# Attention with a gated layer behind it: remainder blocks as 64x64 tiles, the layer's products in scaled float16 halves, the row sums folded into the probabilities, and a new order

## The chip, the cores and the metric

The kernel runs on one core of one Trainium2 chip. The metric is device microseconds (us) of one execution, as the median of several runs. The engines are named as the profile names them: PE multiplies matrices and PEld loads its stationary operand, DVE, ACT and POOL work on elements, and SP issues the DMAs. Each engine runs its own list of instructions in the order in which it stands, and waits on semaphores where it needs another engine's result.

## What is computed

Eight batches, eight heads, 576 positions, head size 64, all float32:

```python
scores = scale * np.matmul(q, k.transpose(0, 1, 3, 2))
psi_rel = np.log1p(np.abs(pos[:, None] - pos[None, :]))
psi_i = np.log1p(np.maximum(pos[:, None], 1.0))
bias = np.maximum((psi_rel / psi_i)[..., None] @ w1 + b1, 0.0) @ w2   # one per head, the same in every batch
attn = softmax(scores + bias)            # rows minus their maximum; 1e-9 is added to each row sum
x = concat over heads of attn @ v        # (8, 576, 512)
gate = sigmoid(causal convolution of x over 5 positions, a weight for each channel)
out = (gate * (x @ w_val)) @ w_out
```

## The kernel before

The work is cut into 32 *pairs*: two heads of one batch. One pair has 1152 rows of scores, in four blocks of 128 positions by two heads, and a *remainder* block for the last 64 positions of both heads.

**A block.** `qkm` (L623) makes the scores on PE with four float32 products that use 64 rows of the array each, two beside each other. `logits` (L665) adds the bias on DVE and takes the row's extreme. `expo` (L677) takes the exponential on ACT and sums the rows. From there a pair goes one of two ways, set by a string of T and D, `TRANS`:

- T: DVE turns the sums into reciprocals (`eps` L701, `recip` L704), `norm` (L722) multiplies the probabilities with them on POOL or DVE, PE transposes them in float32 (`tp`, L762), ACT or DVE copies them out of PSUM, and float32 products with v follow (`piece`, L832).
- D: `top` (L245 on ACT, L249 on POOL) rounds the probabilities to float16, `rest` (L252) subtracts that to get the low half, a transposing DMA (L796) turns both round, and float16 products with v follow (also L832, three for one). The reciprocals come in afterwards: `rb` (L881; L914 for the remainder) spreads them over PSUM with a product, and `mu` (L891, L925) multiplies the result with them on DVE.

12 of the 32 pairs are T, 20 are D. `LDWEIGHTS` rows are PE's loads of the stationary operand.

**The remainder.** `qkr` (L635) multiplies a stationary operand that is block diagonal for the two heads (zeros are loaded with q and k) with 640 columns of k, so that half of the products are with zeros. Its bias tile has -1e30 in the places that are not wanted. DVE, ACT and POOL then work on 640 columns, 576 of which matter.

**The bias** is computed once in the first 65 us, in 36 strips of 16 rows (`relu` L346 on DVE and L344 on ACT, `bias_mm` L365 on PE, `bias_fin` L384/L386), written to DRAM, and loaded again as skewed tiles. Only the tiles of four heads lie in SBUF at a time. So the pairs run as: heads 0-3 of batches 0-3; heads 4-7 of all batches in the order 0, 4, 1, 5, ...; heads 0-3 of batches 4-7. The bias is loaded three times, and the half of a batch's x that is made long before the other goes to DRAM (`xs`, L928) and back (L955).

**The gated layer** of a batch runs when both its halves are there: the convolution (L1009, L1018; for the last batch L968 to L983), the sigmoid (L1030), then in two parts of 256 and 320 positions `split_hi`/`split_lo` of x into a float32r high and low half, `val` (L1075, three products for one), `gf` (L1085: times the gate), `ghi`/`glo`, `outp` (L1132, three products for one), `ote` (copy out of PSUM) and the store. The weights are read as float64 bits and rebuilt on DVE (L454 to L484) after the bias stage.

**What sets the order.** Every step is a task with a list of engines that could do it, a cost for each, and a priority: the pair's place times `PER`, plus an offset from a table (`PAIR_AT`, `MLP_AT`, `OFFS` by the step's name). A planner takes the tasks by these numbers, its own costs and the number of buffers (`BUFS`), and writes one fixed list for each engine.

```python
t3 = add([("A", 0.77)], expo, [t2], h + 1)
t4 = tp_ = add([("A", 0.58), ("V", 0.38), ("G", 0.66)], top, [t3, tp_ if a else None], h + 1.2, ...)
t5 = add([("G", 1.25), ("V", 0.68)], rest, [t4], h + 2, (), [eb])
```

Here A, V and G are ACT, DVE and POOL, the figures are the planner's costs, and the list after the function holds what the task waits for.

Of the kernel before, what the change touches and what calls it, by code (L numbers as in the profile page):

```python
# [39 lines left out]
RUNS = ((0, (0, 1, 2, 3)), (1, (0, 4, 1, 5, 2, 6, 3, 7)), (0, (4, 5, 6, 7)))  # L40
MLP_STEPS = 33
MLP_AT = (27, 17, 14, 9, 8, 19, 12, 70)
PAIR_AT = (1, 3, -1, 0, -0.5, -1, 2.5, -2.5, -4.5, -5, -0.5, -0.5, -0.5, 0.5, 2.5, -1.5, -2, -2.5, -2, 1.5, 1.5, 1, -2.5, -0.5, -1.5, -5, -5.5, -7, 0, 3, 0.5, 0.5)
TRANS = tuple(x == "T" for x in "TTTDTTTTDTTDDTDDDDDTDDTDDDDDDDDD")
BUFS = dict(w=13, d=5, pt=2, sp=2, ps=4, qk=2, rel=4, be=6, xp=2, xh=1, gh=1, gx=1)
RING = dict(er="w", hlr="w", raw="w", e="d", hl="d", xo="w", vt="w", ptr="w", gate="w", gf="w", ot="w", tt="ps", po="ps", pm="ps", cv="ps")
LOOK = dict(w=14.02, ps=60.04, d=6.72, be=3.8, gh=227.3, pt=9.76, xh=21.35, sp=1.22, xp=0.44)
# [13 lines left out]
PARTS = ((0, 256), (256, 320))  # L61
LEAST = float(np.array([0x38000000], np.uint32).view(np.float32)[0])
# [16 lines left out]
class Plan:  # L79
# [6 lines left out]
    def __init__(self, bufs):  # L86
        self.tasks, self.bufs = [], bufs

    def add(self, engines, fn, deps=(), pri=0.0, takes=(), uses=(), hold=0.5):
        pri += OFFS.get(getattr(fn, "func", fn).__name__, 0.0)  # L90
# [3 lines left out]
        name = getattr(fn, "func", fn).__name__  # L94
# [110 lines left out]
def attention_gated_mlp(  # L205
# [23 lines left out]
    for k in set(BUFS) & {"sp", "ps", "w", "d", "pt", "qk"}:  # L229
# [20 lines left out]

    def sub(e, out, in0, in1):
# [176 lines left out]
    users_of_bias = {}  # L428

    def load_bias(run, hg, l, c, pri):  # L430
# [3 lines left out]
        def bias_ld(e):  # L434
            if c < NM:
                SP.dma_start(biasm[l][c], bias_rows_of(c, 2 * p, 2))
            else:
                SP.dma_start(biasr[l][0:REM, 0:S], bias_rows_of(c, 2 * p, 1))
                SP.dma_start(biasr[l][REM:P, REM:RW], bias_rows_of(c, 2 * p + 1, 1))

        deps = stored[c] + users_of_bias.get((run - 1, l, c), [])
        return add([("S", 1.65 if c < NM else 0.9)], bias_ld, deps, pri)


    def double(b, raw, n):
        mp = pools["mp"]
# [787 lines left out]
```

## Time and profile before

| | |
|---|---|
| median of 3 runs | 747.57 us (747.43 to 747.65) |
| the profiled execution, span | 748.5 us |
| PE busy | 704.3 us, 94% |
| DVE busy | 583.9 us, 78% |
| ACT busy | 575.0 us, 77% |
| POOL busy | 481.9 us, 64% |
| SP's DMA queue | 83.6% of 16 DMA engines' span |
| granted TensorE clock, mean | 0.990 |

A row of the groups reads: line, engine, operation, what is written and read, shapes, how many | busy us of the group, mean ns of one | idle time of the engine just before them, and what ended most of it. A float32 product is two records for one instruction. Busy time of an engine is a union: instructions that overlap count once.

### The profile page before, as it was taken

How to read it: one execution, taken by the hardware profiler on the slowest of the kernel's cores; microseconds unless marked ns; L12 is line 12 of the kernel's file. 1: busy time of each engine (PE TensorE's matmuls, PEld its weight loads, DVE VectorE, ACT ScalarE, POOL GpSimd, SP SyncE). 2: the span in 40 equal slices, each digit the busy share in tenths (PEclk: the TensorE clock that was granted, in tenths of full speed). 3: DMA queues.
4: the chain of work that ended last, by engine and by line, in shares of the span. 5: the costliest groups of instructions: out<-in, count | busy, mean ns of one | idle time of the engine just before them, and what ended most of it. 6: DMA issues, size and time to landing. Idle time of an engine off the chain costs nothing.

```text
span 748.5 us, 17263 instructions
## 1 busy us (share of the span) xinstructions
PE 704.3 (94%) x6122; PEld 498.4 (67%) x6122; DVE 583.9 (78%) x1590; ACT 575.0 (77%) x1277; POOL 481.9 (64%) x553
## 2 busy tenths in 40 slices
PE   5768999999989999999999999999999899999997
PEld 2214666666566666687687677767777678688886
DVE  6996698988879979988588768977579889897431
ACT  6988577777778997898677976797767988985632
POOL 1003369556767866699874695668787787876842
PEclk9989999999999999999999999999999999999999
DMA  8888248569893897899999689899999999996211
GB/s 274 280 267 270 80 151 190 146 193 281 170 228 104 145 201 185 177 199 211 224 212 212 140 184 231 259 247 194 235 221 194 226 247 208 198 170 133 71 48 51
DMA packets 273221, 143.23 MB, mean 191 GB/s; under 512 B 243312, under 2 KB 243568, under 8 KB 273136
## 3 DMA queue, kind: packets, MB, share of 16 engines
q1 hardware_dynamic: 272992, 141.84, 83.6%
q8 instruction: 48, 0.79, 0.4%
q10 hardware_dynamic: 144, 0.29, 0.2%
q14 instruction: 37, 0.30, 0.1%
HBM read 56.77 MB, written 25.05 MB: 109 GB/s over the span
## 4 chain that ended last, share of the span: by engine, by line
PE 57%; DMA 12%; DVE 12%; ACT 10%; issue 4%; POOL 3%; SPq 0%; POOLq 0%; ACTq 0%; DVEq 0%
PE t_sp L623 13%; PE t_ps L832 11%; PE t_ps L1132 11%; PE t_ps L1075 9%; DMA t_pt<-t_d 6%; PE t_ps L762 4%; PE t_sp L635 4%; DVE t_d L665 3%; DMA bias_d<-t_be 3%; DVE t_ps L1018 3%; ACT t_d L677 2%; PE t_ps L904 2%; DMA t_w<-vd 1%; PE t_ps L881 1%; DVE rel L346 1%
## 5 line engine op out<-in xcount | busy, mean ns | idle before, releaser
L677 ACT ACTIVATE t_d<-t_d,nm 128x576 f32<-128x576 f32 x256 | 197.8, 774 | 56.9 <-DVE nm L665 54.9
L252 POOL TENSOR_TENSOR t_d<-t_d 128x576 f16<-128x576 f32 x160 | 209.8, 1324 | 45.7 <-ACT t_d L245 37.6
L665 DVE CUSTOM_DVE_ANT_0 t_d<-t_sp,bias 128x576 f32<-128x576 f32 x256 | 188.2, 750 | 22.1 <-PE t_sp L623 10.4
L623 PE MATMUL t_sp<-t_qk 64*128 64x288 f32 x1024 | 174.7, 431 | 6.1 <-DVE nm L665 5.5
L832 PE MATMUL t_ps<-t_pt,t_w 128*64 128x256 f16 (+1 forms) x1680 | 141.7, 309 | 5.0 <-DMA t_pt<-t_d 3.7
L722 POOL TENSOR_SCALAR t_d<-t_d,rinv 128x576 f32<-128x576 f32 x96 | 72.8, 769 | 106.5 <-DVE rinv L704 58.6
L623 PEld LDWEIGHTS t_sp<-t_qk 64*128 64x128 f32 x1024 | 99.0, 186 | 55.1 <-issue 17.4
L1018 DVE SCALAR_TENSOR_TENSOR t_ps<-t_xp,convw,t_ps 128x288 f32<-128x288 f32 x168 | 86.9, 518 | 3.4 <-ACT t_ps L1009 0.8
L1075 PE MATMUL t_ps<-xh,wv 128*128 128x320 f32 (+1 forms) x512 | 83.4, 300 | 0.2 <-ACT t_pt L245 0.2
L245 ACT CAST t_d<-t_d 128x576 f16<-128x576 f32 x113 | 75.1, 669 | 6.6 <-POOL t_d L252 3.0
L832 PEld LDWEIGHTS <-t_w 128*64 128x64 f16 x1200 | 61.1, 109 | 25.0 <-issue 22.2
L1075 PEld LDWEIGHTS t_ps<-xh,wv 128*128 128x128 f32 x512 | 71.6, 188 | 8.5 <-issue 4.7
L1132 PE MATMUL t_ps<-wo,gh 128*128 128x512 f32 x256 | 71.0, 409 | 1.0 <-ACT gh L245 1.0
L762 PE MATMUL t_ps<-ident,t_d 128*128 128x128 f32 x432 | 62.7, 280 | 2.5 <-POOL t_d L722 0.9
L762 PEld LDWEIGHTS t_ps<-ident,t_d 128*128 128x128 f32 x432 | 47.0, 140 | 23.5 <-issue 8.3
L245 ACT COPY t_pt<-t_ps 128x512 f32<-128x512 f32 (+1 forms) x98 | 48.6, 516 | 11.4 <-PE t_ps L762 11.2
L1132 PEld LDWEIGHTS t_ps<-wo,gh 128*128 128x128 f32 x256 | 45.3, 188 | 16.2 <-issue 4.3
L365 PE MATMUL t_ps<-rel,w 128*32 128x288 f32 (+17 forms) x352 | 40.4, 525 | 14.6 <-ACT t_be L384 11.6
L1085 DVE TENSOR_TENSOR t_w<-t_ps,t_w 128x256 f32<-128x256 f32 (+1 forms) x64 | 28.5, 452 | 30.7 <-PE t_ps L1075 28.2
L252 POOL TENSOR_TENSOR gl<-t_w,gh 128x256 fp32r<-128x256 f32 x52 | 39.6, 762 | 19.4 <-ACT gh L245 15.8
L245 ACT COPY t_w<-t_ps 128x512 f32<-128x512 f32 (+2 forms) x64 | 31.8, 503 | 22.0 <-PE t_ps L1132 20.7
L677 ACT ACTIVATION_READ_ACCUMULATOR t_d<-t_d,nm 128x1 f32 x256 | 48.6, 190 | 0.0
(115 smaller groups left out, 1167.5 us busy)
## 6 DMA issues: line engine op xcount, KB each, us to landing
t_qk<-qkd SPq DMA_DIRECT2D x32, 640.0 KB, 4.7
bias<-bias_d SPq DMA_DIRECT2D x24, 576.0 KB, 4.8
bias_d<-t_be SPq DMA_DIRECT2D x36, 295.5 KB, 4.6
out<-t_w SPq DMA_DIRECT2D x32, 256.0 KB, 2.6
t_w<-vd SPq DMA_DIRECT2D x20, 320.0 KB, 3.9
xs<-t_w SPq DMA_DIRECT2D x16, 288.0 KB, 3.4
t_xp<-xs SPq DMA_DIRECT2D x8, 576.0 KB, 4.6
t_w<-vn SPq DMA_DIRECT2D x12, 320.0 KB, 5.2
```

The lines of the kernel that those rows point to most:

```text
L245: A.copy(out=out, in_=in_)
L252: (V if e == "V" else G).tensor_tensor(out=out, in0=in0, in1=in1, op=ALU.subtract)
L365: T.matmul(pb[32 * g : 32 * g + 32, 0 : y - x], lhsT=w28, rhs=rel[g].t[:, x:y], start=True, stop=True, tile_position=(0, 32 * g),)
L623: T.matmul(ts[a][:, j, 0:hw], lhsT=qk.t[r, c * P : (c + 1) * P], rhs=qk.t[r, x : x + hw], start=True, stop=True,)
L665: V.tensor_tensor_reduce(out=part().rearrange("p (j f) -> p j f", j=2), in0=sp.t[:, :, 0 : w // 2], in1=bias.rearrange("p (j f) -> p j f", ...
L677: A.activation(out=part(), in_=part(), func=AF.Exp, bias=nms[c][:, a : a + 1], scale=-1.0, accum_out=sums[c][:, a, 0:1],)
L722: (G if e == "G" else V).tensor_scalar(out=t, in0=t, scalar1=rinvs[c][:, a : a + 1], scalar2=1.0, op0=ALU.mult, op1=ALU.mult,)
L762: T.transpose(t[:, k * P : (k + 1) * P], es[c].t[:, (k0 + k) * P : (k0 + k + 1) * P], ident)
L832: T.matmul(po.t[r, 0:256], lhsT=vt.t[:, v0 + t, r], rhs=pt[:, w, :, :] if tr else pt[:, :, w, :], start=(k == 0), stop=(k == 5 * len(prods ...
L1018: V.scalar_tensor_tensor(out=o, in0=x, scalar=cw, in1=t, op0=ALU.mult, op1=ALU.add)
L1075: T.matmul(pm.t[:, 0:w], lhsT=pools["wv"][wi][:, k, d * P : (d + 1) * P], rhs=xb.t[xi][:, k, 0:w], start=(q == 0 and k == 0), stop=(q == 2 ...
L1132: T.matmul(pm.t, lhsT=gb.t[gi][:, k, o : o + P] if o < 256 else gx.t[gi][:, k, :], rhs=pools["wo"][wi][:, k, :], start=(q == 0 and k == 0) ...
```

## The change

Five things change together.

1. **Remainders.** The remainders of the two pairs that are neighbours (same batch, four heads) form one block of 128 rows: rows 0-63 for the first pair, 64-127 for the second. `qkr` makes it with eight 64x64 products, four for each half of the columns, each with its own place in the array. From then on it is a block of 576 columns like the others; the block-diagonal zeros, the -1e30 and all 640-column steps of the scores go.
2. **Reciprocal inside the split.** In a D pair `eps` and `recip` now come straight after the exponentials, `top` multiplies with the reciprocal as it rounds, and `rest` multiplies and subtracts: one instruction on DVE, two on POOL (L262, L263), and only POOL is listed. `rb` and `mu` go. `eps` may run on POOL (L771).
3. **The gated layer in float16.** Both operands are scaled with powers and maxima so that two float16 halves hold them. New: a maximum over every v tile (L620, L634), a trip of one value per partition through DRAM for each batch (L1010, L1014), one for the weights (L568, L572), scales in `split_hi` (ACT with a scale, L1132), `split_lo` (now DVE only, L1137), `gf` (L1177) and `ote` (L1241), and a row maximum with scales on the rebuilt weights (L532 to L541). float16 products need their own LDWEIGHTS in the list.
4. **Bias resident, batches in turn.** The bias tiles of all eight heads stay in SBUF. After batches 0 and 1 (interleaved) every batch is done with all heads before the next. `xs` and the reloads go; the gated layer of batch 0 can start after pair 5.
5. **Order.** All planner numbers are new. `TRANS` has one letter for two pairs, 18 pairs are now T and 14 D; the weights are rebuilt during and right after the bias stage; `BUFS` changes (w 13 to 12, d 5 to 6, qk 2 to 3).

```diff
-RUNS = ((0, (0, 1, 2, 3)), (1, (0, 4, 1, 5, 2, 6, 3, 7)), (0, (4, 5, 6, 7)))
+RUNS = ((0, (0, 1)), (1, (0, 1))) + tuple((hg, (b,)) for b in range(2, 8) for hg in range(2))
-TRANS = tuple(x == "T" for x in "TTTDTTTTDTTDDTDDDDDTDDTDDDDDDDDD")
+TRANS = tuple(x == "T" for x in "TTTTDTDDTDTDTDTD")
-BUFS = dict(w=13, d=5, pt=2, sp=2, ps=4, qk=2, rel=4, be=6, xp=2, xh=1, gh=1, gx=1)
+BUFS = dict(w=12, d=6, pt=2, sp=2, ps=4, qk=3, rel=3, be=8, xp=2, xh=1, gh=1, gx=1)
...
-                t, hw = new(sps[0], [P, 2, 512], F32), RW // 2
+                ts, hw = [new(sp, [P, 2, 512], F32) for sp in sps], S // 2
                 for j in range(2):
-                    T.matmul(t[:, j, 0:hw], lhsT=qk.t[:, NM * P : QW], rhs=qk.t[:, QW + j * hw : QW + (j + 1) * hw], ...)
+                    for a, r in enumerate(halfs):
+                        for m, o in zip(both, halfs):
+                            q = m["qk"].t
+                            x = S + j * hw
+                            T.matmul(ts[a][o, j, 0:hw], lhsT=q[r, NM * P : S], rhs=q[r, x : x + hw], ...)
...
-                        copy(e, hl.t[:, 0, :] if c == NM else hl.t[:, 0, a, :], part())
+                        o, i, x = hl.t[:, 0, a, :], part(c, a), rinvs[c][:, a : a + 1]
+                        if e == "A":
+                            A.activation(out=o, in_=i, func=AF.Copy, scale=x)
...
-                        sub(e, f(1), part(), f(0))
+                        scaled(e, hl.t[:, 1, a, :], part(c, a), rinvs[c][:, a : a + 1], hl.t[:, 0, a, :], ALU.subtract)
...
-                    t5 = add([("G", 1.25), ("V", 0.68)], rest, [t4], h + 2, (), [eb])
+                        moved[c, x] = add([("G", 2.0)], partial(rest, a=x), [tp_], h + 1 + x, (), [eb])
...
+    def scaled(e, out, in0, s, in1, op):
+        if e == "V":
+            V.scalar_tensor_tensor(out=out, in0=in0, scalar=s, in1=in1, op0=ALU.mult, op1=op)
+        else:
+            G.tensor_scalar(out=in0, in0=in0, scalar1=s, scalar2=1.0, op0=ALU.mult, op1=ALU.mult)
+            G.tensor_tensor(out=out, in0=in0, in1=in1, op=op)
...
-            x = add([("P", 0.44)], rb, [last, rsum[g]], d + 1.2, (), [po])
-            x1 = add([("V", 0.34)], mu, [x0, x], d + 2, (), [po])
+            x1 = x0
...
-                        xb.t = [pools["mp"].tile([P, NK, 320], F32R, name=x, tag=x) for x in ("xh", "xl")]
+                        xb.t = [pools["mp"].tile([P, NK, 320], F16, name=x, tag=x) for x in ("xh", "xl")]
...
-                u = add([("V", 0.38), ("G", 0.75)], split_lo, [h], base + 0.3 * k + 0.2, (), [xp])
+                u = add([("V", 0.38)], split_lo, [h], base + 0.3 * k + 0.2, (), [xp])
...
-                    copy(e, ot.t, pm.t)
+                    x = bsc[:, b, 0:1] if o < 256 else oscx[:, b_pair : b_pair + 1]
+                    if e == "A":
+                        A.activation(out=ot.t, in_=pm.t, func=AF.Copy, scale=x)
```

Three places show what this does to the lists.

DVE in the first half of the bias stage, before (`rel` is `relu`, `t_be` is `bias_fin`):

```order
L346 TENSOR_SCALAR rel<-gt,sct,nb_129 128x464 x3
L346 TENSOR_SCALAR rel<-gt,sct,nb_129 128x448 x3
L346 TENSOR_SCALAR rel<-gt,sct,nb_129 128x432 x3
L346 TENSOR_SCALAR rel<-gt,sct,nb_129 128x416 x3
L386 TENSOR_SCALAR t_be<-t_ps,cadd 128x464
L346 TENSOR_SCALAR rel<-gt,sct,nb_129 128x400 x3
L346 TENSOR_SCALAR rel<-gt,sct,nb_129 128x384 x3
```

The same place after the change (L522 ends the rebuilding of the convolution's weights, L620 is the maximum over a v tile):

```order
L620 TENSOR_REDUCE vcol<-t_w 128x1
L369 TENSOR_SCALAR rel<-gt,sct,nb_142 128x464 x3
L369 TENSOR_SCALAR rel<-gt,sct,nb_142 128x448 x3
L369 TENSOR_SCALAR rel<-gt,sct,nb_142 128x432 x3
L522 TENSOR_TENSOR convw<-t_w 128x20
L620 TENSOR_REDUCE vcol<-t_w 128x1
L369 TENSOR_SCALAR rel<-gt,sct,nb_142 128x416 x3
L369 TENSOR_SCALAR rel<-gt,sct,nb_142 128x400 x3
L369 TENSOR_SCALAR rel<-gt,sct,nb_142 128x384 x3
L620 TENSOR_REDUCE vcol<-t_w 128x1
```

Maxima over v and steps of the weights' rebuilding (eight of 512 columns follow before the last strip) have moved in between the strips.

POOL in a D pair between two T pairs, before (`t_d` 128x576 on L252 is `rest`, on L722 `norm`):

```order
L252 TENSOR_TENSOR t_d<-t_d 128x576 x2
L252 TENSOR_TENSOR xl<-t_xp,xh 128x320 x2
L252 TENSOR_TENSOR t_d<-t_d 128x576 x2
L722 TENSOR_SCALAR t_d<-t_d,rinv 128x576 x2
L252 TENSOR_TENSOR t_w<-t_w 128x640
```

POOL at such a place after the change (L771 is `eps`, L820 `top`, L262 and L263 the two steps of `rest`, L799 `norm`):

```order
L771 TENSOR_SCALAR rinv<-sm_162 128x2
L262 TENSOR_SCALAR t_d<-t_d,rinv 128x576
L263 TENSOR_TENSOR t_d<-t_d 128x576
L262 TENSOR_SCALAR t_d<-t_d,rinv 128x576
L263 TENSOR_TENSOR t_d<-t_d 128x576
L820 TENSOR_SCALAR t_d<-t_d,rinv 128x576
L262 TENSOR_SCALAR t_d<-t_d,rinv 128x576
L263 TENSOR_TENSOR t_d<-t_d 128x576
L799 TENSOR_SCALAR t_d<-t_d,rinv 128x576 x2
```

Each low half is now two instructions on POOL; the low halves of x (`xl`) have left POOL.

ACT after the last remainder's copy (L922) at the end of the program, before:

```order
L922 ACTIVATE t_xp<-t_ps,vsc 128x64
L972 ACTIVATE t_w<-t_xp,convw 128x576
L245 CAST xh<-t_xp 128x320 x3
L245 COPY t_w<-t_ps 128x512
L245 CAST gh<-t_w 128x256
L245 COPY t_w<-t_ps 128x512
L245 CAST gh<-t_w 128x256 x2
L972 ACTIVATE t_w<-t_xp,convw 128x576
L978 ACTIVATE t_w<-t_xp,convw 128x576
L245 COPY t_w<-t_ps 128x512
```

The same place after the change (L975 is that copy, L1053 and L1059 the convolution, L1241 `ote`, L1111 the sigmoid):

```order
L975 ACTIVATE t_xp<-t_ps,vsc 128x64
L1053 ACTIVATE t_w<-t_xp,convw 128x576
L1241 ACTIVATE t_w<-t_ps,bsc 128x512
L1111 ACTIVATE t_w<-t_w 128x576
L1059 ACTIVATE t_w<-t_xp,convw 128x576
L1241 ACTIVATE t_w<-t_ps,bsc 128x512
L1059 ACTIVATE t_w<-t_xp,convw 128x576 x2
L249 CAST gh<-t_w 128x256
```

Less of the batch before the last is left to stand beside the last convolution: two output copies, where before a whole part of it and five copies followed.

More of the change, by code (lines that the diff above doesn't have):

```diff
@@ L506, in cw, with w_max, w_scale, w_inv @@
                 )
-            return add([("V", 0.1)], cw, [t], pri)
+            return add([("V", 0.1)], cw, [t], pri, (), tmp)
+        m = ("wv", "wo").index(hi_lo)
+        wm, wt, wi = (x[:, m, k : k + 1] for x in wrow)
+        def w_max(e):
+            V.tensor_reduce(out=wm, in_=b["a"].bitcast(F32), op=ALU.max, axis=AX.X, apply_absolute_value=True)
+        def w_scale(e):
+            scalars(e, wt, wm, 1e-30, 2.0**-12, ALU.max)
+        def w_inv(e):
+            V.reciprocal(out=wi, in_=wt)
@@ new lines, in attention_gated_mlp, with wg_store, wg_load, wg_max @@
+    last = WEIGHTS[0] + 9 * WEIGHTS[1]
+    wall, wallb = {}, Buf("wall")
+    def wg_store(e):
+        SP.dma_start(wbd, wrow[1].rearrange("p m k -> p (m k)"))
+    def wg_load(e):
+        wall["t"] = new(wallb, [P, P * 2 * NK], F32)
+        SP.dma_start(wall["t"], wbd.rearrange("p c -> (p c)").partition_broadcast(P))
+    def wg_max(e):
+        t = wall["t"].rearrange("q (p m k) -> q m p k", m=2, k=NK)
+        V.tensor_reduce(out=wsc[:, 0:2], in_=t, op=ALU.max, axis=AX.XY)
+    def wg_inv(e):
+        V.reciprocal(out=wsc[:, 2:4], in_=wsc[:, 0:2])
@@ L530, in attention_gated_mlp @@
     spilled, arrived, taker = {}, {}, {}
+    maxima = {}
+    mates = {}
     def pair(n):
@@ L611, in pair, with part, block @@
         hls = {}
-        for c in range(NM + 1):
-            w = S if c < NM else RW
-            sps = [Buf("sp") for _ in range(2 if c < NM else 1)]
+        mine = mates[n] = dict(qk=qk, loaded=loaded, vt=vt, tv=tv)
+        both = [mates[n - 1], mine] if l else None
+        ptr = Buf("ptr")
+        def part(c, a):
+            return es[c].t[:, a * S : (a + 1) * S]
+        def block(c):
+            exps = {}
+            sps = [Buf("sp") for _ in range(2)]
             def qkm(e, c=c, sps=sps):
@@ L703, in recip @@
+                    o = rinvs[c] if tr else sums[c][:, 1, :, 0]
+                    V.tensor_reduce(out=o, in_=sums[c][:, 0], op=ALU.add, axis=AX.X)
+                    if not tr:
+                        V.tensor_reduce(out=rinvs[c], in_=sums[c][:, 1], op=ALU.mult, axis=AX.X)
                 def recip(e, c=c):
-                    V.reciprocal(out=inv[c], in_=inv[c])
-                t1 = qkt
-                bl = bias_task.get((run, l, c))
+                    V.reciprocal(out=rinvs[c], in_=rinvs[c])
@@ new lines, in rest @@
+                    def rest(e, a, c=c, hl=hl):
+                        scaled(e, hl.t[:, 1, a, :], part(c, a), rinvs[c][:, a : a + 1], hl.t[:, 0, a, :], ALU.subtract)
+                    tp_ = None
+                    for x in range(2):
+                        tp_ = add(
+                            [("A", 0.66), ("V", 0.38), ("G", 0.75)],
+                            partial(top, a=x),
+                            [tr_, tp_],
+                            h + 0.2 + x,
+                            [hl] if x == 0 else (),
+                        )
+                        moved[c, x] = add([("G", 2.0)], partial(rest, a=x), [tp_], h + 1 + x, (), [eb])
```

511 lines of the change are left out of this document (269 added, 242 removed).

## The prediction

> **What bounds the kernel now.** I read the page's busy shares first, then a table of three stretches (bias stage, middle, tail), then PE's waits.
>
> ```profile
> span 748.5 us, 17263 instructions
> PE 704.3 (94%) x6122; PEld 498.4 (67%) x6122; DVE 583.9 (78%) x1590; ACT 575.0 (77%) x1277; POOL 481.9 (64%) x553
> ```
>
> ```profile
> core 0: us, PE busy (x) PEld busy (x) DVE busy (x) ACT busy (x) POOL busy (x), PEclk, DMA share, GB/s
> 0.00:65.00 65.00, 44.71 (x390) 14.22 (x392) 55.39 (x139) 54.72 (x115) 5.14 (x31) 0.95 0.88 282
> 65.00:690.00 625.00, 606.57 (x5455) 439.14 (x5452) 511.25 (x1429) 497.23 (x1112) 446.99 (x486) 0.99 0.90 195
> 690.00:748.50 58.50, 53.01 (x283) 45.06 (x281) 17.22 (x24) 23.03 (x51) 29.80 (x38) 0.99 0.16 54
> ```
>
> ```profile
> PE t_ps L365 <- ACT t_be L384: 11.6, 15, 1.9
> PE t_sp L623 <- DVE nm L665: 5.5, 8, 1.3
> PE t_ps L832 <- DMA t_pt<-t_d: 3.7, 8, 0.8
> PE t_sp L635 <- DVE nm L665: 3.1, 4, 1.3
> PE t_ps L904 <- DVE t_xp L891: 1.0, 1, 1.0
> ```
>
> The middle is PE's: it is busy 606.57 of 625 us, and its 18.4 idle us are scattered. DVE, next, has 511.25, which is 82%. In the first 65 us DVE and ACT lead (85% and 84%) and PE sits idle for 20.3 us; in the tail PE leads again, idle for 5.5. PE idles 44.2 us in all, and time comes off this kernel mainly as PE work. The span is 0.9 us above the median of the runs shown (747.57), so I sum against 748.5 and take 0.9 off at the end.
>
> **PE, part by part.** The groups that the change touches:
>
> ```profile
> L623 PE MATMUL t_sp<-t_qk 64*128 64x288 f32 x1024 | 174.7, 431 | 6.1 <-DVE nm L665 5.5 <-DMA t_qk<-qkd 0.2
> L635 PE MATMUL t_sp<-t_qk 128*128 128x320 f32 x128 | 42.7, 457 | 3.1 <-DVE nm L665 3.1
> L832 PE MATMUL t_ps<-t_pt,t_w 128*64 128x256 f16 x1200 | 77.9, 275 | 5.0 <-DMA t_pt<-t_d 3.7 <-DVE xh L247 1.1
> L832 PE MATMUL t_ps<-t_pt,t_w 128*64 128x256 f32 x480 | 63.9, 395 | 0.0
> L762 PE MATMUL t_ps<-ident,t_d 128*128 128x128 f32 x432 | 62.7, 280 | 2.5 <-POOL t_d L722 0.9 <-ACT t_pt L245 0.6 <-DVE t_xp L891 0.3
> L762 PE MATMUL t_ps<-ident,t_w 128*128 128x128 f32 x60 | 9.8, 277 | 0.4 <-DVE t_pt L247 0.3
> L881 PE MATMUL t_ps<-ident,rinvs 128*64 128x128 f32 x320 | 24.3, 273 | 0.0
> L914 PE MATMUL t_ps<-ident,rinvs 128*64 128x64 f32 x80 | 6.3, 236 | 0.0
> L904 PE MATMUL t_ps<-t_w 128*64 128x64 f16 (+1 forms) x840 | 22.8, 206 | 1.1 <-DVE t_xp L891 1.0
> ```
>
> - Remainder scores. Before, 32 pairs at 42.7/32 = 1.33 us. After, 16 blocks of eight 64x64 products. No row shows four tiles at work; the nearest is L623, where two row tiles overlap: 174.7 us for 128 blocks, 1.36 each. If the four overlap as the two do, a remainder block costs that: 16 x 1.36 = 21.8, **-20.9 us**. If only two overlap it costs twice that, 43.7, and +1.0. I take the first, since L832 and L365 (128*64 and 128*32) also show tiles in use beside each other.
> - Products with v in D pairs: 14 for 20, 77.9 x 14/20 = 54.5, **-23.4**. In T pairs 18 for 12, 63.9 x 18/12 = 95.9, **+32.0**.
> - Transposes on PE: 729 for 492, (62.7 + 9.8) x 729/492 = 107.4, **+34.9**.
> - `rb` goes: **-30.6** (24.3 + 6.3). The remainder's products with v (L904, 22.8) change in mix alone, under 1 us: **+0.8**, if D's third goes (13.3 of it) and T's half comes on top.
> - The layer in float16. The pace is read from start to start in one quiet stretch:
>
> ```profile
> 596.54 1.83 PE L832 MATMUL t_ps<-t_pt,t_w 128*64 128x256 f16 x30
> 598.21 0.60 PE L881 MATMUL t_ps<-ident,rinvs 128*64 128x128 f32 x8
> ...
> 605.01 2.03 PE L1132 MATMUL t_ps<-wo,gh 128*128 128x512 f32 x8
> 606.88 1.09 PE L1132 MATMUL t_ps<-wo,gl 128*128 128x512 f32 x4
> 607.81 1.33 PE L1075 MATMUL t_ps<-xh,wv 128*128 128x320 f32 x8
> 608.98 0.75 PE L1075 MATMUL t_ps<-xl,wv 128*128 128x320 f32 x4
> ```
>
>   Float32r: 1.87 us for eight of 512 columns, 0.457 ns a column; 1.17 for eight of 320, the same. Float16: 1.67 us for 30, two beside each other, so 111 ns for 256 columns, 0.435 a column with the entry into the run. There are 432 products of 512 columns and 384 each of 320 and 256, 442 thousand columns: 0.022 ns each is -9.9 us. That is one end. The other is the busy times, 65 ns for one float16 product and so 130 for 256 columns, against 153 for float32r by this kernel's own union, -15% of about 249 us, -37. I take **-13**, near the pace.
>
> The Trainium skill's page TensorE: Matmul & The Clock Gate (Back-to-back issue gap) gives columns over 2.4 plus 2.5 ns for a warm product, and with 0.419, 0.424 and 0.427 ns a column this would be some 15 us less instead of 13. Its page TensorEngine Tiling (Array Packing), section Key Properties, says that a change of tiling drains the array; the groups on PE fall from 533 to 467, 60 of them `rb` that is priced above, so that this adds nothing to the sum here.
>
> Together: -20.9 - 23.4 + 32.0 + 34.9 - 30.6 + 0.8 - 13 = **-20.2 us** of PE work, 704 to 684.
>
> **The other engines.** DVE's prices:
>
> ```profile
> L346 DVE TENSOR_SCALAR rel<-gt,sct,nb 128x576 f32<-128x576 f32 x6 | 3.4, 627 | 0.0
> L247 DVE CAST t_d<-t_d 128x576 f16<-128x576 f32 x6 | 4.8, 797 | 4.3 <-ACT t_d L677 4.1
> L252 DVE TENSOR_TENSOR gl<-t_w,gh 128x256 fp32r<-128x256 f32 x12 | 8.2, 686 | 5.6 <-ACT gh L245 5.6
> L1018 DVE SCALAR_TENSOR_TENSOR t_ps<-t_xp,convw,t_ps 128x288 f32<-128x288 f32 x168 | 86.9, 518 | 3.4 <-ACT t_ps L1009 0.8
> L566 DVE TENSOR_REDUCE vsc<-t_w 128x1 f32<-128x640 f32 x20 | 16.2, 812 | 3.8 <-DMA t_w<-vd 3.8
> L891 DVE TENSOR_TENSOR t_xp<-t_xp,t_ps 128x256 f32<-128x256 f32 x28 | 11.6, 416 | 10.5 <-ACT t_xp L861 10.4
> ```
>
> In: 44 `norm` at 0.63 to 0.80 (+28 to +35), 32 more low halves `gl` (+22), 64 low halves of x at about 0.55 where 26 stood before (+15), 12 more maxima over v (+10), row maxima, scales and trips of the weights and batches (about 60 small ones and 15 of 512 columns, +18). Out: 60 `mu` (40 at 0.416, 20 small: -21), a third of the v splits and fewer copies from PSUM (-13). About 175 instructions more in all. Sums of single durations overcount, since neighbours overlap a little, so I take **+67**: 584 to 651, between +45 and +85. ACT gains about 60 copies of 512 columns out of PSUM for the T pairs, +35. Neither is on the path while PE is, but DVE's cover gets thin: in the middle it would have 511 + 67 - 10 (bias stage) - 6 (tail) = 562 us of some 605, 93%.
>
> POOL's own:
>
> ```profile
> L252 POOL TENSOR_TENSOR t_d<-t_d 128x576 f16<-128x576 f32 x160 | 209.8, 1324 | 45.7 <-ACT t_d L245 37.6
> L722 POOL TENSOR_SCALAR t_d<-t_d,rinv 128x576 f32<-128x576 f32 x96 | 72.8, 769 | 106.5 <-DVE rinv L704 58.6
> ```
>
> 126 `rest` at 0.77 + 1.32 = 2.09 (263), 118 `norm` (91), some 70 small and 45 others (75): about 430 of 482. Within a D block it is 4.2 us where a block has 605/144 = 4.2 us of the middle on average; T blocks need 1.5. Only batch 3 has two D groups in a row. The softer spot is the row's delay: probabilities now reach the transposing DMA about 2 us later (reciprocal, and 0.77 more a half), which D's sixth `d` buffer covers.
>
> DMA: 77 transposing DMAs for 120, no `xs`, a third less bias. The wait for it (3.7) should shrink, the wait for `mu` (1.0) goes: **-4** with L635's.
>
> Bias stage: DVE is handed five maxima over v (4.1 us), eight steps of the weights (about 4) and small ones, some 10 us into 9.6 idle ones. The cost lies between 0 and +10; **+3**, since ACT, as long as DVE here, gets nothing. Tail: before, part of the batch before the last stands between the last remainder and the last batch's products; now less, with convolution and sigmoid of two quarters in front. Between 0 and +6 (PE's tail idles 5.5 now), **+1**. DVE's crowding in the middle: between 0 and +45 (below), **+2** here.
>
> Sum: 748.5 - 20.2 - 4 + 3 + 1 + 2 = 730.3; less 0.9, **729 us**.
>
> **Rivals.**
> - DVE keeps the pace at the density that it can hold. The stretches in which it is densest:
>
> ```profile
> 300.00:325.00 25.00, 24.73 (x186) 17.23 (x186) 24.32 (x62) 20.50 (x47) 18.91 (x20) 1.00 0.90 184
> 200.00:325.00 125.00, 119.69 (x1077) 83.00 (x1076) 109.48 (x313) 104.91 (x239) 88.31 (x94) 1.00 0.84 175
> ```
>
>   For: over 125 us it never passed 88%; at that, 562/0.88 = 639 us of middle, plus 68 and 59 less 0.9, gives **765**, slower. Against: in 25 us it reached 97% with PE at 99%, so its gaps are PE's doing. It decides once DVE cannot hold 91% (562/0.91 = 618: 744).
> - The same in part: DVE at 92%, 611 us of middle, **737**, still faster.
> - Tiles: the four 64x64 products overlap only two by two. Then +21.9, **751**; against it, the two kinds of tiles of L623 and L832 each overlap.
> - Tighter: PE's idle in the middle halves (-9), float16 gives the -15 to -37 side (-8), the bias stage costs nothing (-3): **709**.
>
> **Numbers.** Likeliest, PE at today's density: 0.45, 729, by itself 720 to 735. DVE in part 0.20 (735 to 744), DVE slower 0.14 (746 to 780), tighter 0.14 (700 to 719), tiles 0.04, other 0.03. The range leaves out the far ends of the slow and the tight case, a tenth each: 706 to 758. Within 0.2% of 747.6 (1.5 us, about what a measurement of this kernel can tell from none) lie 0.04, of DVE's and the tiles' cases; faster 0.80; slower 0.16.
>
> **What would show it.** Right: PE about 684 us busy, L720's group near 22 us, no `rb`, L1229's eight products of 512 columns in 1.72 to 1.78 us, DVE near 650 with PE still at 95% or more of the middle. Wrong: PE below 93% of the middle with waits for DVE's `nm` or for `t_d` from POOL at the top of its list; a bias stage beyond 75 us; L720 at 40 us.

## The result, and the profile after

The changed kernel takes 796.63 us (median of 4 runs, 795.23 to 799.43), 1.067 times the kernel before (95% interval 1.0645 to 1.0700): 49 us slower, where 18.6 us faster was forecast and 758 was the upper end. Medians of the kernel before lie between 745.7 and 748.9 from chip to chip, so each experiment below is read by its ratio on its own chip.

The page's first lines, and the three stretches (bias stage, middle, tail; columns as before):

```profile
span 795.0 us, 16857 instructions
PE 707.8 (89%) x5907; PEld 439.1 (55%) x5907; DVE 635.8 (80%) x1764; ACT 607.5 (76%) x1343; POOL 448.2 (56%) x605
```

```profile
0.00:70.00 70.00, 54.26 (x405) 20.21 (x406) 63.78 (x163) 60.56 (x130) 12.14 (x57) 0.98 0.85 279
70.00:735.00 665.00, 600.91 (x5061) 386.76 (x5062) 536.37 (x1528) 512.59 (x1145) 418.81 (x532) 0.95 0.58 128
735.00:795.00 60.00, 52.66 (x445) 32.16 (x443) 35.65 (x75) 34.36 (x72) 17.27 (x17) 0.99 0.29 73
```

PE idles 87.2 us where it idled 44.2, and the granted clock of the middle is 0.95 for 0.99. From the trace's clock record and PE's intervals: the clock stood at one half in spells of 3.4 to 13.7 us, and PE was busy for 52.2 us of them (13.2 before), so 26.1 us of work were lost to it (6.6 before). So the difference of the spans splits up: idle +43.0, clock +19.5, PE's work at full clock (707.8 - 26.1 against 704.3 - 6.6) -16.0; together +46.5, which is 795.0 - 748.5. **PE's work went down, and waiting ate the gain almost three times over.** No engine became the bound: DVE is at 80%, and the DMA queue's share fell from 83.6% to 57.3%.

The groups that answer to those shown of before:

```profile
L704 PE MATMUL t_sp<-t_qk 64*128 64x288 f32 x1024 | 186.9, 450 | 31.1 <-DVE nm L747 24.3 <-DMA t_qk<-qkd 6.5
L720 PE MATMUL t_sp<-t_qk 64*64 64x288 f32 x256 | 20.4, 415 | 0.0
L912 PE MATMUL t_ps<-t_pt,t_w 128*64 128x256 f32 x720 | 91.4, 388 | 0.3 <-ACT t_pt L249 0.2
L912 PE MATMUL t_ps<-t_pt,t_w 128*64 128x256 f16 x840 | 55.8, 286 | 9.6 <-DMA t_pt<-t_d 6.7 <-ACT t_d L249 1.9 <-DVE t_w L1049 1.0
L845 PE MATMUL t_ps<-ident,t_d 128*128 128x128 f32 x729 | 109.1, 286 | 17.0 <-POOL t_d L799 5.4 <-ACT t_pt L249 3.1 <-ACT t_d L249 2.6
```

PE's wait for DVE's logits (`nm` in L704's row) has grown from 5.5 us to 24.3. The list of DVE's own waits says what DVE was doing then:

```profile
DVE bsc L1017 <- DMA vall<-vb: 30.1, 5, 7.6
```

That is the *trip*: for each batch `vb_max` (L1007) takes the maximum over v in every partition, SP stores that column of 128 values to DRAM (L1010, `vb`), loads it back to all partitions (L1014, `vall`), and DVE takes the maximum over it (L1017). One of the stops, in order of time (the rows of other instructions are left out):

```profile
608.09 0.15 DVE L1007 TENSOR_REDUCE bsc<-vcol 128x1 f32<-128x4 f32 x1
608.27 0.33 SPq L1010 DMA_DIRECT2D vb<-bsc  x1
...
615.00 0.33 SPq L1014 DMA_DIRECT2D vall<-vb  x1
615.44 2.27 SPq L667 DMA_TRANSPOSE t_w<-t_w  x1
616.19 0.33 PE L845 MATMUL t_ps<-ident,t_d 128*128 128x128 f32 x1
617.81 6.53 SPq L879 DMA_TRANSPOSE t_pt<-t_d  x2
619.85 0.29 DVE L1017 TENSOR_REDUCE bsc<-vall 128x1 f32<-128x128 f32 x1 [6.28 <-DMA vall<-vb]
621.04 0.75 DVE L747 CUSTOM_DVE_ANT_0 t_d<-t_sp,bias 128x576 f32<-128x576 f32 x1
621.86 1.81 PE L704 MATMUL t_sp<-t_qk 64*128 64x288 f32 x4 [5.34 <-DVE nm L747]
```

The store is issued at 608.27, and nothing follows on SP until it has landed at 615.00; DVE stands at L1017 from 613.6 to 619.85, its logits behind it, and PE starves for 5.3 us. PE then restarts at half clock, as the same place in short stretches shows (the last three numbers: PEclk, DMA share, GB/s). The queue is all but empty in the first two stretches, so nothing stands in front of the store: it is slow by itself.

```profile
608.40:611.80 3.40, 3.38 (x27) 1.82 (x23) 2.68 (x9) 3.40 (x8) 3.29 (x3) 1.00 0.02 0
611.80:615.20 3.40, 3.40 (x28) 2.10 (x28) 1.73 (x6) 3.09 (x7) 2.89 (x4) 1.00 0.06 5
615.20:619.60 4.40, 1.32 (x11) 0.57 (x7) 0.00 (x0) 0.00 (x0) 2.48 (x3) 0.99 0.22 38
619.60:623.00 3.40, 1.14 (x4) 0.90 (x6) 2.93 (x14) 1.16 (x3) 0.00 (x0) 0.50 1.15 253
623.00:626.40 3.40, 3.40 (x11) 1.49 (x9) 2.76 (x10) 2.75 (x6) 2.08 (x3) 0.50 0.85 160
626.40:629.80 3.40, 3.40 (x51) 1.97 (x51) 3.19 (x11) 3.04 (x7) 2.71 (x4) 1.00 0.04 10
```

11 products in a stretch of 3.4 us, all of it busy, and 51 in the one behind it, though of other kinds. The Trainium skill's page TensorE: Matmul & The Clock Gate (Part 1: The HAM clock gate) says that PE runs at half its clock after about one idle window of 3.4 us, and at the full one after a busy window; the spells here are multiples of 3.41 us at 0.50, but for one that the program's end cuts off, which agrees.

### The profile page after: what moved, and what is told of

Read it like the earlier page. It is cut to its first block, busy times and chain, and to the rows that moved or that the text cites. A ratio compares the mean times of both kernels' runs of the same rounds, so it can differ in the third digit from the quotient of the medians.

```text
span 795.0 us, 16857 instructions
## 1 busy us (share of the span) xinstructions
PE 707.8 (89%) x5907; PEld 439.1 (55%) x5907; DVE 635.8 (80%) x1764; ACT 607.5 (76%) x1343; POOL 448.2 (56%) x605
## 3 DMA queue, kind: packets, MB, share of 16 engines
q1 hardware_dynamic: 194720, 107.50, 57.3%
## 5 line engine op out<-in xcount | busy, mean ns | idle before, releaser
L704 PE MATMUL t_sp<-t_qk 64*128 64x288 f32 x1024 | 186.9, 450 | 31.1 <-DVE nm L747 24.3
L263 POOL TENSOR_TENSOR t_d<-t_d 128x576 f16<-128x576 f32 x126 | 163.5, 1298 | 10.5
L704 PEld LDWEIGHTS t_sp<-t_qk 64*128 64x128 f32 x1024 | 107.0, 195 | 85.8 <-DVE nm L747 38.3
L799 POOL TENSOR_SCALAR t_d<-t_d,rinv 128x576 f32<-128x576 f32 x118 | 96.6, 827 | 78.3 <-DVE rinv L782 38.4
L845 PE MATMUL t_ps<-ident,t_d 128*128 128x128 f32 x729 | 109.1, 286 | 17.0 <-POOL t_d L799 5.4
L262 POOL TENSOR_SCALAR t_d<-t_d,rinv 128x576 f32<-128x576 f32 x126 | 98.8, 784 | 35.9 <-ACT t_d L818 23.9
L845 PEld LDWEIGHTS t_ps<-ident,t_d 128*128 128x128 f32 x729 | 81.3, 144 | 56.7 <-issue 22.0
L249 ACT COPY t_pt<-t_ps 128x512 f32<-128x512 f32 (+1 forms) x172 | 83.3, 517 | 27.3 <-PE t_ps L845 26.4
L1167 PEld LDWEIGHTS <-wv 128*128 128x128 f16 x768 | 73.8, 99 | 30.7 <-issue 10.5
L771 POOL TENSOR_SCALAR rinv<-sm 128x2 f32<-128x2 f32 x65 | 22.8, 350 | 115.8 <-ACT t_d L759 113.9
L818 ACT ACTIVATE t_d<-t_d,rinv 128x576 f16<-128x576 f32 x108 | 81.2, 767 | 7.9 <-DVE rinv L782 3.3
L1167 PE MATMUL t_ps<-xh,wv 128*128 128x320 f16 (+1 forms) x512 | 77.2, 290 | 0.8 <-DVE t_pt L251 0.6
L1229 PE MATMUL t_ps<-wo,gh 128*128 128x512 f16 x256 | 64.5, 390 | 2.4 <-ACT gh L249 1.7
L912 PEld LDWEIGHTS t_ps<-t_pt,t_w 128*64 128x64 f32 x720 | 46.4, 137 | 34.6 <-issue 10.4
L1177 DVE SCALAR_TENSOR_TENSOR t_w<-t_ps,gsc,t_w 128x256 f32<-128x256 f32 (+1 forms) x64 | 32.5, 512 | 20.6 <-PE t_ps L1167 15.4
```

The costliest lines, as they stand in the source:

```text
L249: A.copy(out=out, in_=in_)
L262: G.tensor_scalar(out=in0, in0=in0, scalar1=s, scalar2=1.0, op0=ALU.mult, op1=ALU.mult)
L263: G.tensor_tensor(out=out, in0=in0, in1=in1, op=op)
L704: T.matmul(ts[a][:, j, 0:hw], lhsT=qk.t[r, c * P : (c + 1) * P], rhs=qk.t[r, x : x + hw], start=True, stop=True,)
L799: (G if e == "G" else V).tensor_scalar(out=t, in0=t, scalar1=rinvs[c][:, a : a + 1], scalar2=1.0, op0=ALU.mult, op1=ALU.mult,)
L818: A.activation(out=o, in_=i, func=AF.Copy, scale=x)
```

## The experiments

**First round: what does the trip cost?** Theory A: DVE's wait at L1017 stops the chain. Rival B: the new order is too dense, above all on DVE, and the trip only takes slack that would be lost anyhow.

*fixed_scale*, the changed kernel with DVE's wait alone taken away:

```diff
-            V.tensor_reduce(out=bsc[:, b, 1:2], in_=got["t"], op=ALU.max, axis=AX.X)
+            V.tensor_reduce(out=bsc[:, b, 1:2], in_=ident, op=ALU.max, axis=AX.X)
```

> Theory A (the batch's trip blocks DVE): DVE's row maximum over the batch's maxima (L1017) no longer waits for the DMA; it reads a constant tile, so the scale of x is a constant instead of the batch's maximum. Order, DMAs and every other instruction stay. PE's five gaps behind L1017 go (6.45, 6.67, 5.34, 6.42 and 1.06 us, 25.9), and so does the work lost while the granted clock stood at one half after four of them (4.02, 3.61, 4.51 and 5.88 us of busy PE at 0.5, 9.0): 796.6 - 35 = 762, between 752 and 772, with a mean clock of 0.97. Rival B (DVE and POOL are too crowded in the new order, and the trip only takes slack that would be lost anyhow): PE's waits for DVE come back elsewhere, 785 to 797.

789.26 us, ratio 1.055 (1.052 to 1.059): of the 49 us, 7 by the medians and 9 by the ratios. Theory A's number failed and B's held. But SP's list of waits names something that B does not speak of:

```profile
SPq L1014 <- DMA vb<-bsc: 37.6, 5, 7.8
```

*trip_pe*, the trip replaced by one product on PE:

```diff
-            SP.dma_start(vbd[b].rearrange("(p c) -> p c", c=1), bsc[:, b, 0:1])
...
-            SP.dma_start(got["t"], vbd[b].partition_broadcast(P))
+            T.matmul(bank(vbb)[:, 0:P], lhsT=bsc[:, b, 0:1].to_broadcast([P, P]), rhs=ident, start=True, stop=True)
```

> The batch's maxima are spread by one product with the identity into a PSUM bank, as rb did for the reciprocals, in place of the store to DRAM and the load from it; result as in the changed kernel. The order is planned anew with that one task, so that it differs in many places. Theory A: as the constant scale, and SP's queue no longer stands behind the store's landing (6.5 us, eight times): 745 to 765. Rival B: 780 to 800.

767.71 us, ratio 1.027 (1.024 to 1.031), just above A's range and far from B's. The whole trip is worth more than DVE's wait for it, though this order is a new one.

*before_trips*, eight trips put into the kernel before, whose order they leave alone:

```diff
+        if gone < 8 and t.on == "S" and t.start >= at[gone]:
+            SP.dma_start(vbd[gone].rearrange("(p c) -> p c", c=1), scr[:, 0:1])
+            vall[gone] = smp.tile([P, P], F32, name="vall", tag="vall", bufs=2)
+            SP.dma_start(vall[gone], vbd[gone].partition_broadcast(P))
...
+        if back < gone and t.on == "V" and t.start >= at[back] + 4.5:
+            V.tensor_reduce(out=scr[:, 1:2], in_=vall[back], op=ALU.max, axis=AX.X)
```

> The kernel before in its order, with eight trips added, 75 us apart: a store of one column, a load of it to all partitions, and on DVE a maximum over what was loaded, 4.5 planned us behind the store, as in the changed kernel; nothing uses it. Theory A: each trip stops DVE and then PE for some 6 us and halves the clock for 3.4 to 6.8 us behind it, 8 us in all; with some of the eight covered 40 to 65 us, 788 to 812. Rival B (PE's buffers cover a wait of that size): 748 to 758.

824.06 us, ratio 1.100 (1.095 to 1.106), more than either forecast: 9.4 us a trip by the ratio. The trip is dear in the order before too, where DVE had slack (82% busy in the middle).

*before_f16*, one part of the change alone (`F32R` to `F16` in five places of the kernel before):

```diff
-                        xb.t = [pools["mp"].tile([P, NK, 320], F32R, name=x, tag=x) for x in ("xh", "xl")]
+                        xb.t = [pools["mp"].tile([P, NK, 320], F16, name=x, tag=x) for x in ("xh", "xl")]
```

> The kernel before in its order, the gated layer's halves of x, weights and gated product as float16 tiles in place of float32r, without any scales (precision is lost, the number of products is the same). The prediction's term: PE 13 us less by pace (0.435 for 0.457 ns a column; the changed kernel's quiet stretch shows 0.422, which would be 15), so 733 to 738. By the busy times of single products, 37 less: 711. Rival: the time comes back as waits for DVE, 745 to 748; or each product's own weight load costs more than the faster product brings, 748 to 755.

737.64 us, ratio 0.986 (0.983 to 0.990): 10 us less, at the upper end of the range by pace; the rivals fell, and this version takes less time than both kernels, by 1.4% and more. It has no scales, so its halves hold only what float16 holds.

**Second round: the trip, DVE's wait or SP's queue?** Theory A2: SP's load stands behind the landing of its own store, and with it all that is queued behind it. Theory C: what is left above the forecast comes from the order and from the T pairs' chain.

*no_trip* is fixed_scale without the two DMAs:

```diff
-            SP.dma_start(vbd[b].rearrange("(p c) -> p c", c=1), bsc[:, b, 0:1])
...
-            SP.dma_start(got["t"], vbd[b].partition_broadcast(P))
```

> The changed kernel in its order with the constant scale, and now without the store and the load of the batch's maxima as well. With the constant scale alone 789.3 us were measured: the load waits on SP's queue for its own store to land (37.6 us in five waits of 7.8 at most), and what is queued behind it there (loads of q and k, transposing DMAs) starts late. Theory A2 (the trip's second half of the price is SP's queue): 768 to 778, with the gap of 7.2 us near 151 and the two near 460 and 560 gone. Rival B (crowding; SP's queue has slack): 785 to 790.

751.21 us, ratio 1.002 (0.999 to 1.005), far below B's range and 17 us below A2's too. The trip with all that hangs on it costs 45 us by the medians (49 by the ratios); without it the changed kernel is level with the kernel before. PE's idle falls from 87.2 to 54.6 us and the work lost to the clock from 26.1 to 9.2:

```profile
span 750.5 us, 16834 instructions
PE 695.9 (93%) x5907; PEld 432.1 (58%) x5907; DVE 639.1 (85%) x1764; ACT 607.1 (81%) x1343; POOL 447.4 (60%) x605
```

*trip_pe_less_dve* and *before_less_dve* leave out two taps of the convolution, in trip_pe and in the kernel before:

```diff
                     for tp in tps:
+                        if tp in (1, 2):
+                            continue
```

> The kernel with the maxima spread on PE (767.7 us) in its order, without two of the five taps of the convolution in seven batches (not computed): 112 products on DVE of 0.517 us, 58 us, go. Theory B (what is left above the forecast comes from DVE's density): 740 to 752. Rival C (it comes from the order itself: what stands where on PE, the copies on ACT, the transposing DMAs): 760 to 768.

> The same 112 products left out of the kernel before, in its order. Both theories: PE bounds it and DVE has slack, 740 to 748. Only if DVE were already on the path before would it fall under 735.

761.35 us, ratio 1.019 (1.011 to 1.027), 6 us less than trip_pe and in rival C's range; and 744.76, ratio 0.996 (0.993 to 1.000), 3 less than before by the ratio. DVE's density explains a few us, not the loss.

*before_trips_late* moves DVE's maximum to 25 planned us behind the store:

```diff
-        if back < gone and t.on == "V" and t.start >= at[back] + 4.5:
+        if back < gone and t.on == "V" and t.start >= at[back] + 25:
```

> The kernel before with the eight trips, but DVE's maximum comes 25 planned us behind the store instead of 4.5, so that what it reads has landed. SP's load still waits for its store to land. Of the 76.5 us that the trips cost (824.1 against 747.5) the part that is left is SP's. Theory A2: 755 to 785. If the whole price was DVE's wait: 747 to 752.

822.13 us, ratio 1.099 (1.093 to 1.106). Nobody waits for the load any more, and the price is the same. That is above A2's range as well, which had given part of the price to DVE's wait. SP's waits and PE's in this run:

```profile
SPq L1183 <- DMA vb<-scr: 65.3, 8, 8.9
```

```profile
PE t_sp L623 <- DVE nm L665: 45.9, 17, 9.7
PE t_ps L904 <- DMA t_w<-t_w: 10.5, 1, 10.5
```

In one of the longest of these stops, near 290 us, DVE's logits are late because ACT's rounding waits 9.4 us for a transposing DMA that SP issued behind the trip's load. This speaks for SP's side, as A2 has it, but not for A2's number.

**Third round: each wait alone.** *stale_scale* (the changed kernel) and *before_trips_apart* (the kernel before) keep both DMAs, but load what the trip before had stored, so that SP has no landing to wait for:

```diff
-            SP.dma_start(got["t"], vbd[b].partition_broadcast(P))
+            SP.dma_start(got["t"], vbd[max(b - 1, 0)].partition_broadcast(P))
```

> The changed kernel in its order with all its DMAs, but the load of the maxima reads what the batch before had stored (the first batch its own), so that SP's queue has no landing to wait for; the scale of x is then that of the batch before. DVE still waits for its load. Theory A2 (SP's queue carries the price): 750 to 760 against 796.6 for the changed kernel and 751.2 without any trip. If DVE's wait for the load had a price of its own, some 3 to 5 us at each of five places: 765 to 780.

> The kernel before with the eight trips and DVE's maximum 4.5 planned us behind, but each load reads what the trip before had stored. The same DMAs and the same wait of DVE, without SP's wait for a landing. Theory A2: of the 76 us that the trips cost no more than 10 are left, 748 to 758. Theory A (DVE's wait): 790 to 825.

791.75 us, ratio 1.060 (1.055 to 1.066); and 806.08, ratio 1.078 (1.072 to 1.084). Both miss A2 by 30 us or more. The second lies in A's range (DVE's wait), the first above its other range. DVE still waits for the load in both (19.6 us in five waits, 35.1 in seven). With SP free the transposing DMAs are issued earlier, and yet little gets through. The stretches of one stop of stale_scale, whose store was issued at 608.0 and landed 9.6 us later (last columns: DMA share, GB/s):

```profile
611.00:613.00 2.00, 1.99 (x17) 1.18 (x17) 1.93 (x8) 2.00 (x5) 1.84 (x2) 1.00 0.83 157
613.00:615.00 2.00, 2.00 (x18) 1.23 (x20) 0.30 (x1) 1.62 (x4) 1.62 (x2) 1.00 1.83 63
615.00:617.00 2.00, 1.25 (x11) 0.53 (x7) 0.00 (x0) 0.00 (x0) 1.92 (x3) 1.00 0.39 3
617.00:619.00 2.00, 0.00 (x0) 0.00 (x0) 0.92 (x7) 0.00 (x0) 0.49 (x1) 1.00 1.01 95
619.00:621.00 2.00, 1.01 (x4) 0.57 (x6) 2.00 (x8) 1.03 (x3) 0.00 (x0) 1.00 1.27 287
```

Up to 613 the queue still moves 157 GB/s. From 613 on transposing DMAs and the load are under way and it moves 63 and then 3 GB/s, until the store has landed. That made theory D: the store itself, 128 pieces of four bytes, holds up the queue.

*true_latency* keeps the trip and gives the planner 5 us more for each of its DMAs:

```diff
-                t.end = bus + 0.75
+                t.end = bus + 0.75 + (5.0 if t.name in ("vb_store", "vb_load") else 0.0)
```

> The changed kernel, result and all, planned anew with 5 us more for each of the trip's two DMAs, as the trace has them: one or more other DMAs now stand between the store and its load on SP's queue, and DVE's maximum comes later. Theory A2: 755 to 772, near the 767.7 of the kernel with the maxima spread on PE, which was planned anew too. If the order matters little and the trip is hidden in full: 748 to 755.

791.03 us, ratio 1.060 (1.055 to 1.065): a miss for both. Planning for the landing took away DVE's wait for the load and two thirds of SP's for the store (11.9 us in three waits, where the changed kernel has 33.1 in five), and brought 6 us. The order is a new one here too, so this alone does not settle it; D has a reason for so small a gain.

*no_trip_no_norm* leaves out the multiplications of the T pairs:

```diff
                     def norm(e, a, c=c):
+                        return
```

> The changed kernel without the trip (751.2 us), and without the products that normalise the probabilities of the T pairs (118 on POOL, 44 on DVE; the T pairs' rows stay unnormalised). PE waits 13.2 us in front of the T pairs' transposes there, before the change 2.9. Theory C (what is left above the forecast is the T pairs' longer chain from the exponential over POOL to the transpose): 738 to 746. Rival: the waits go to the copies out of PSUM or to DVE's logits, 748 to 752.

743.24 us, ratio 0.994 (0.991 to 0.997), as theory C had it.

**Fourth round: the store itself.** *before_trips_free* is the kernel before with the eight trips' DMAs, for which nobody waits (the edits of before_trips_apart and before_trips_late together):

> The kernel before with the eight trips' DMAs, each load reading what the trip before had stored, and DVE's maximum 25 planned us behind: no one waits for either DMA. Theory D (the store of 128 pieces of four bytes stalls the DMA queue, and the transposing DMAs and loads behind it land late): 780 to 810. Theory A2+A (two waits, each enough alone): 747 to 755.

793.65 us, ratio 1.064 (1.058 to 1.070). Theory D, and the other is out: 6.0 us a trip with no one waiting for it. The DMA list and PE's waits (the DMAs that are late are those that PE and its suppliers need):

```profile
vall<-vb SPq DMA_DIRECT2D x8, 64.0 KB, 8.5
vb<-scr SPq DMA_DIRECT2D x8, 0.5 KB, 9.0
```

```profile
PE t_sp L623 <- DVE nm L665: 23.8, 14, 6.3
...
PE t_ps L832 <- DMA t_pt<-t_d: 8.2, 5, 5.2
PE t_ps L904 <- DMA t_w<-t_w: 7.2, 2, 5.8
```

*before_row_free* and *before_row_trips* store the same 512 bytes as one row of one partition, the first with no waits, the second with both:

```diff
-            SP.dma_start(vbd[gone].rearrange("(p c) -> p c", c=1), scr[:, 0:1])
+            SP.dma_start(vbd[gone].rearrange("(p c) -> p c", p=1), row)
```

> The same row store, with no one waiting for either DMA. Both theories: 747 to 752. If it stays above 770, the load to all partitions is what stalls the queue, not the store.

> The kernel before with the eight trips and both waits, as in the run that took 824.1 us, but the store writes 512 bytes from one partition in place of four from each of 128. Theory D: the store lands in 2 to 3 us, SP and DVE wait for less, 750 to 775. Theory A2+A: the waits are nearly as long, 800 to 825.

751.55 us, ratio 1.006 (1.003 to 1.010); and 756.67, ratio 1.014 (1.010 to 1.019). A trip falls from 6.0 to 0.6 us without waits, and from 9.4 to 1.3 with them. So the load to all partitions is innocent, and the store's small pieces are the cause. SP still waits for the row to land, but 13.8 us in eight waits and not 65.3. The trip's 10.0% in before_trips splits into 6.4 for the two DMAs with no one waiting (0.6 of which the row store has too), and 3.5 more for SP's wait (before_trips_late) or 1.4 more for DVE's (before_trips_apart); these add up to 11.3, so the two waits seem to overlap.

*no_trip_less_dve* cuts the two taps in no_trip:

> The changed kernel without the trip (751.2 us), without the 112 products of the convolution (58 us of DVE, not computed). The same cut was worth 4 us in the kernel before and 6 in the one planned anew. Theory B (DVE's density makes the 22 us left above the forecast): 732 to 742. Theory C (the T pairs' chain, whose multiplications alone were worth 8): 744 to 749.

742.84 us, ratio 0.996 (0.993 to 0.998): 5 us less by ratio, 3 of which the kernel before gains as well. Theory C's range missed by 1 us, B's too.

**Fifth: the cause in the changed kernel.** Its list of DMAs holds the contrast by itself; `wb` is the weights' trip, 128 pieces of 32 bytes:

```profile
vall<-vb SPq DMA_DIRECT2D x8, 64.0 KB, 4.8
t_d<-wb SPq DMA_DIRECT2D x1, 512.0 KB, 3.6
vb<-bsc SPq DMA_DIRECT2D x8, 0.5 KB, 7.2
...
wb<-wrow SPq DMA_DIRECT2D x1, 4.0 KB, 1.4
```

*after_wide* gives the batch's trip the same pieces, in the same order of instructions and with the trip's value kept (the load is eight times as large, and has one buffer for two):

```diff
-            V.tensor_reduce(out=bsc[:, b, 0:1], in_=vcol[:, b], op=ALU.max, axis=AX.X)
+            V.tensor_reduce(out=wide, in_=vcol[:, b].unsqueeze(1).to_broadcast([P, 8, NP]), op=ALU.max, axis=AX.X)
...
-            SP.dma_start(vbd[b].rearrange("(p c) -> p c", c=1), bsc[:, b, 0:1])
+            SP.dma_start(vbd[b].rearrange("(p c) -> p c", c=8), wide)
```

> The changed kernel in its order, with its trip and its result: each partition's maximum is written eight times side by side, so that the store has 128 pieces of 32 bytes in place of four, the load brings eight times as much (512 KB over all partitions), and DVE reads every eighth value. Theory D (pieces of four bytes stall the queue): the store lands in some 1.4 us and the load in some 3.7, as the weights' two do, which the order's 4.5 us nearly cover: 750 to 760, near the 751.2 without any trip. If a trip is dear whatever its pieces: 780 to 797.

759.62 us, ratio 1.016 (1.012 to 1.020). Eight times the bytes, and 37 us less. Some 8 us are left above no_trip; DVE still waits 6.5 us for the load, SP 5.6 for the store.

```profile
vb<-wide SPq DMA_DIRECT2D x8, 4.0 KB, 1.4
```

*no_trip_light* leaves out both the T pairs' multiplications and the two taps:

> The changed kernel without the trip, without the T pairs' 162 multiplications and without the convolution's 112 products (neither computed). If the waits for the element engines are what is left above the forecast, the two add up: 733 to 738, at 0.983 of the kernel before. If both took the same waits: 741 to 744, 0.993. PE's idle time tells it too: 54.6 us without the trip, near 40 if they add up.

736.24 us, ratio 0.983 (0.980 to 0.987), the number for adding up. The sign in PE's idle time did not come: it is 49.6 us of 738.6, not near 40, and PE's busy time fell instead, by 6.9 us. (The profiled execution is the longest of the six, 740.42 us.)

```profile
span 738.6 us, 16354 instructions
PE 689.0 (93%) x5907; PEld 427.6 (58%) x5907; DVE 570.4 (77%) x1608; ACT 604.5 (82%) x1343; POOL 348.1 (47%) x487
```

## Why the prediction was wrong

**The step that failed** is the one on DMA ("77 transposing DMAs for 120, no `xs`, a third less bias", -4), together with the list of DVE's new work, where the "scales and trips of the weights and batches" stand among 60 small instructions. The trip was priced as what DVE does in it, well under a microsecond (0.15 and 0.29 us in the rows of the stop above). Its two DMAs were counted on no queue, its wait was put behind nothing, and no rival held it. It cost 45 us (796.6 against 751.2) of the 67.6 by which the forecast was missed, and 37 of the 45 go when the store's pieces are 32 bytes (after_wide). The price holds the stop of the DMA queue behind a store of 512 bytes in 128 pieces, SP's and DVE's waits for that store and its load, and PE's halved clock after most of the stops. The queue's stop is the largest part in the kernel before, where it was run alone (6.4 of 10.0%); in the changed kernel the parts were not separated. That DMAs became fewer and the queue's share fell said nothing on it.

**The priced terms for PE held, one unpriced did not.** Busy times of after, against the forecast: remainder scores 20.4 (21.8; the four tiles do overlap, rival out), products with v in D pairs 55.8 (54.5) and in T pairs 91.4 (95.9), transposes 109.1 (107.4), `rb` gone. The layer: eight float16 products of 512 columns take 1.73 us from start to start (1.72 to 1.78 was named):

```profile
760.62 1.89 PE L1229 MATMUL t_ps<-wo,gh 128*128 128x512 f16 x8
762.35 0.38 PE L1229 MATMUL t_ps<-wo,gl 128*128 128x512 f16 x1
```

That is 0.422 ns a column for 0.457, 15 us, where 13 was taken. (The prediction's 0.419 for 512 columns is a slip, its own rule gives 0.422; the 15 us there stand.) Alone in the kernel before it brought 10. PE's work at full clock fell by 16.0 where 20.2 was forecast; in no_trip, with the same products, by 11.0 (695.9 - 9.2 against 697.7), so this sum is known to some 5 us. One group that was left at its old price grew: the scores of the main blocks (L704) take 181.9 us in no_trip where 174.7 stood, at nearly the same mean (435 and 431 ns), so fewer of them overlap. The elements' engines were near too: DVE 635.8 (651), ACT 607.5 (about 610), POOL 448.2 (about 430).

**The term for crowding was too small.** Without the trip 751.2 is 22 us above the forecast. The spans split these up (750.5 against the sum's 730.3): PE's work fell by 11.0 and not 20.2, which is 9.2; idle time rose by 10.4 where the sum had 2, which is 8.4; the clock took 2.6. DVE's crowding stood at +2 with bounds of 0 and 45. Cutting 162 multiplications and 112 convolution products is worth 14 us by ratio (1.002 to 0.983), 3 of which the kernel before gains for the products alone. So about half of the 22 us hangs on element work, part of it on POOL and the T pairs' chain, where the prediction looked at DVE alone. Only part of it shows as PE's idle time; why PE's busy time falls with it (L704's to 176.6 us in no_trip_light) is not shown. In front of the transposes PE waited 2.9 us before, and in no_trip it waits for POOL's `norm` above all:

```profile
L845 PE MATMUL t_ps<-ident,t_d 128*128 128x128 f32 x729 | 107.8, 285 | 13.2 <-POOL t_d L799 5.4 <-ACT t_pt L249 3.4 <-DVE t_d L799 1.8
```

In time that lies between the rivals "DVE in part" (737) and "DVE slower" (765), by another road. DVE as the bound is not what happened: it has 536.4 of 665 us in the middle. What the rest of the 22 us is stays open, as does how much another order would save: trip_pe, planned anew, is 16 us slower than no_trip.

**Signs that were named.** PE fell under 93% of the middle (600.9 of 665, 90%) with waits for `nm` on top of its list: that was the mark of "wrong", and it was put down to DVE's pace. The same mark has two causes, and only DVE's own waits tell them apart.

## What to carry to other kernels

Price a trip through DRAM by what stands behind it on three lists: the DMA queue itself, the issuing engine's queue, and the engine that takes the result. Store per-partition values in pieces of 32 bytes, not of four, or as one row if they lie in one partition, or spread them with a product on PE; here the wider pieces alone were worth 37 us of 797. And when a wait is taken away and little happens, look for the next one beside it: here DVE's wait, SP's wait and the queue's stop stood beside each other, and with either wait taken away most of the price stayed.

## What was not expected of the hardware

A store of 128 pieces of four bytes from 128 partitions to DRAM lands 6.7 to 12.1 us after its issue, whether or not anything waits for it; 128 pieces of 32 bytes land in 1.4 to 3.0, six of eight in after_wide in 1.4. The narrow store's packets are recorded soon after its issue (141 packets from 607 to 609 in the stop of stale_scale above), so most of its time passes behind them. Before it has landed, DMAs issued behind it on the same queue come to a stop (157 GB/s from 611 to 613, then 63, then 3 from 615 to 617). The Trainium skill's page DMA: Bandwidth & Descriptors (Anatomy of one DMA — SWDGE (gpsimd) path) puts the fixed cost of a DMA on GpSimd's path near 2 us, most of it the receipt of the write. SP issues the stores here; the wide one is near that figure, the narrow one is not, and the measurement decides. Why the narrow one is slow the traces do not show. Neither pieces between 4 and 32 bytes nor another queue were tried.
